# Where attention's softmax is divided by its sum: on the product with the values, or on the exponentials themselves, from the seventh pair of heads on

## The chip, the core and the metric

The kernel runs on one core of a Trainium2 chip. The engines of the core are TensorE (PE; its weight loads are listed apart as PEld), VectorE (DVE), ScalarE (ACT), GpSimd (POOL) and SyncE (SP, which here only issues DMAs). Each engine works through its own instructions in order and meets the others at semaphores. The metric is device time in microseconds (us) of one execution.

## The reference: what is computed

Inputs are q, k and v for 4 batches, 8 heads, 768 positions and 64 features. An attention that only sees keys of the same hash bucket comes first:

```python
mask = q_bucket[:, :, :, None] == k_bucket[:, :, None, :]
scores = scale * np.matmul(q, k.transpose(0, 1, 3, 2))
scores = np.where(mask, scores, -1000000000.0)
scores = scores - np.max(scores, axis=-1, keepdims=True)
attn = np.exp(scores)
attn = attn / (np.sum(attn, axis=-1, keepdims=True) + 1e-09)
return np.matmul(attn, v).astype(np.float32)
```

The heads of a batch are then joined to x, 768 by 512, and a feed-forward part follows: relu(x @ w_in), a convolution of three taps along the positions, h * sigmoid(conv), and a product with w_out.

## The kernel before

**Pairs, units, blocks.** Two heads make a pair; there are 16, four to a batch. A pair has 12 units: a unit is 128 queries of one head against all 768 keys. Four units in a row (two query tiles of both heads, 256 queries) make a block, so a pair has three.

**A unit.** On PE `products` (L250) computes the scores s into PSUM; the mask is part of that product. DVE reads s in `maximum` (L260): it clamps, copies to the SBUF tile e and takes each row's maximum; a second, tiny instruction (L262) turns the maximum into the bias st. ACT then writes exp over e in place and accumulates the row sums (`exponential`, L265). Three units later PE transposes e, 128 columns at a time, into a PSUM tile t (`transposes`, L280), and ACT copies t to SBUF as at (`to_sbuf`, L287).

**The values.** Once a block's four units are copied, PE multiplies them with v (`chunk`, L306), 12 products that the trace lists as 24 instructions. That happens in one stage of four, the one given a 7 by `AVS`.

**The division.** It stands behind the product. When a block's last sum is known, DVE adds 1e-9 and takes reciprocals of the block's four sums (`reciprocals`, L270, L271), GpSimd spreads them to a 128x256 tile rec (L274), PE turns rec with two transposes ahead of the values (`spread`, L301), and ACT copies that out of PSUM (`factors`, L311). DVE multiplies the product by it (x, L315), and GpSimd splits x into a rounded part xh (L316) and the rest xl (L317), which the feed-forward part reads.

**The order.** It is written by hand. Stage i of the main loop issues, engine by engine: s of unit i, its maximum, the transposes of unit i-3 and their copy, the exponential of unit i, then values. In this text A, B, C and D are the four stages of a block in the steady part, where D is the one that also carries the values of the block before; A is the first after them. s and t tiles share a ring of three PSUM buffers (tag S): the transposes in stage i take the buffer of s of unit i-1, so they wait for that unit's maximum; s of unit i takes that of the transposes of stage i-2, so it waits for their copy. Tiles e come from a ring of five.

**Around it.** `prepare` splits the next pair's q and k on GpSimd in the course of a pair (hi, L168; bits, L188; lo, L173, listed as R<-R,hi). In the first six pairs DVE, ACT and GpSimd also decode the weights. After pairs 6, 10, 14 and 16 the feed-forward part of one batch runs (`ffn`), with the last block's values inside it (`fill`).

## Time and profile before

| | before |
|---|---|
| median of 3 runs | 766.6 us (763.26 to 768.91) |
| the profiled execution's own time | 764.44 us |
| its span in the trace | 761.6 us |
| PE busy | 722.1 us (95%) |
| ACT busy | 511.9 us (67%) |
| DVE busy | 486.1 us (64%) |
| GpSimd busy | 294.9 us (39%) |
| granted TensorE clock, mean | 0.992 of 2.4 GHz |

The span runs from the first to the last instruction in the trace; 2.8 us of the execution's time lie around it. PE's matmuls are pipelined, and their listed durations overlap: what a matmul costs is read from one start to the next. "Idle before" in a row is the time in which the engine stood still ahead of an instruction, with what ended it behind the arrow.

### The profile page before, as it was taken

How to read it: one execution, taken by the hardware profiler on the slowest of the kernel's cores; microseconds unless marked ns; L12 is line 12 of the kernel's file. 1: busy time of each engine (PE TensorE's matmuls, PEld its weight loads, DVE VectorE, ACT ScalarE, POOL GpSimd, SP SyncE). 2: the span in 40 equal slices, each digit the busy share in tenths (PEclk: the TensorE clock that was granted, in tenths of full speed). 3: DMA queues.
4: the chain of work that ended last, by engine and by line, in shares of the span. 5: the costliest groups of instructions: out<-in, count | busy, mean ns of one | idle time of the engine just before them, and what ended most of it. 6: DMA issues, size and time to landing. Idle time of an engine off the chain costs nothing.

```text
span 761.6 us, 12950 instructions
## 1 busy us (share of the span) xinstructions
PE 722.1 (95%) x4648; PEld 595.3 (78%) x4648; DVE 486.1 (64%) x1032; ACT 511.9 (67%) x954; POOL 294.9 (39%) x325
## 2 busy tenths in 40 slices
PE   5989989888889999999999999999999999999997
PEld 3867767665679987777889988777778998778986
DVE  7789978777857555555546655555546665554663
ACT  5877768777755558777765557777775556775554
POOL 4355765566536221433424421333424421113222
PEclk8999999999999999999999999999999999999999
DMA  4666576484422111445632202256361211000011
GB/s 138 157 181 191 128 195 165 117 230 108 116 50 65 60 42 64 118 123 150 140 105 53 73 1 105 48 147 154 95 174 40 63 42 62 2 1 1 0 43 41
DMA packets 30351, 72.13 MB, mean 95 GB/s; under 512 B 5936, under 2 KB 7504, under 8 KB 30288
## 3 DMA queue, kind: packets, MB, share of 16 engines
q1 hardware_dynamic: 30000, 71.27, 34.7%
q8 instruction: 36, 0.59, 0.3%
q14 instruction: 27, 0.22, 0.1%
q10 hardware_dynamic: 288, 0.05, 0.0%
HBM read 27.40 MB, written 6.29 MB: 44 GB/s over the span
## 4 chain that ended last, share of the span: by engine, by line
PE 69%; DVE 18%; DMA 5%; ACT 3%; issue 2%; POOL 1%; SPq 1%; DVEq 0%; POOLq 0%; ACTq 0%
PE o L365 18%; PE h L335 17%; PE v L306 14%; PE t L280 10%; DVE e L260 9%; PE s L250 9%; DMA R<-in_qk 2%; ACT at L287 2%; DMA k<-R 2%; DVE x L315 1%; PE hash L183 1%; PE v L301 1%; DVE wuo L92 1%; DVE wlo L96 1%; DVE st L262 1%
## 5 line engine op out<-in xcount | busy, mean ns | idle before, releaser
L260 DVE TENSOR_SCALAR_CACHE_REDUCE e<-s 128x768 f32<-128x768 f32 x192 | 182.9, 953 | 108.2 <-PE s L250 100.4
L265 ACT ACTIVATE e<-e,st 128x768 f32<-128x768 f32 x192 | 180.8, 941 | 30.0 <-DVE st L262 22.2
L287 ACT COPY at<-t 128x768 f32<-128x768 f32 x192 | 151.8, 792 | 61.1 <-PE t L280 61.1
L280 PE MATMUL t<-ident,e 128*128 128x128 f32 x1152 | 161.5, 277 | 17.4 <-DVE e L260 15.2
L280 PEld LDWEIGHTS t<-ident,e 128*128 128x128 f32 x1152 | 133.0, 141 | 40.1 <-DVE e L260 33.5
L344 DVE SCALAR_TENSOR_TENSOR ht<-ht,cw 128x384 f32<-128x384 f32 (+1 forms) x128 | 113.9, 890 | 71.1 <-ACT ht L342 67.4
L365 PE MATMUL o<-wo,g 128*128 128x512 f32 x576 | 143.0, 394 | 1.0 <-POOL g L354 1.0
L335 PE MATMUL h<-xh,wi 128*128 128x386 f32 x512 | 142.2, 341 | 1.0 <-ACT ht L340 1.0
L306 PE MATMUL v<-at,v 128*64 128x256 f32 x1152 | 137.0, 383 | 0.0
L354 POOL TENSOR_TENSOR g<-ht,g 128x384 fp32r<-128x384 f32 x64 | 72.0, 1124 | 151.9 <-ACT g L353 120.1
L365 PEld LDWEIGHTS o<-wo,g 128*128 128x128 f32 x576 | 107.3, 188 | 21.9 <-POOL g L354 1.4
L250 PE MATMUL s<-K,Q 128*128 128x384 f32 x384 | 117.5, 387 | 3.7 <-DVE e L260 2.7
L274 POOL TENSOR_SCALAR rec<-sums 128x256 f32<-128x256 f32 x48 | 19.5, 406 | 246.7 <-ACT at L287 146.7
L306 PEld LDWEIGHTS v<-at,v 128*64 128x64 f32 x1152 | 82.0, 137 | 41.2 <-issue 7.9
L250 PE MATMUL s<-k,q 96*128 96x384 f32 x384 | 99.8, 341 | 2.3 <-DVE e L260 2.2
L335 PEld LDWEIGHTS h<-xh,wi 128*128 128x128 f32 x512 | 94.1, 188 | 5.0 <-ACT ht L340 1.5
L347 ACT ACTIVATE ht<-ht 128x384 f32<-128x384 f32 x64 | 33.6, 526 | 90.4 <-DVE ht L344 90.2
L335 PE MATMUL h<-xl,wi 128*128 128x386 f32 x256 | 86.8, 339 | 0.0
L250 PEld LDWEIGHTS s<-K,Q 128*128 128x128 f32 x384 | 58.9, 192 | 34.5 <-issue 19.0
L250 PEld LDWEIGHTS s<-k,q 96*128 96x128 f32 x384 | 71.1, 192 | 3.1 <-ACT q L230 3.1
L348 DVE TENSOR_TENSOR ht<-ht 128x384 f32<-128x384 f32 x64 | 43.4, 679 | 33.7 <-ACT ht L347 33.4
L173 POOL TENSOR_TENSOR R<-R,hi 128x768 fp32r<-128x768 f32 x30 | 58.9, 1964 | 0.7
(70 smaller groups left out, 632.9 us busy)
## 6 DMA issues: line engine op xcount, KB each, us to landing
R<-in_qk SPq DMA_DIRECT2D x15, 768.0 KB
K<-hi SPq DMA_DIRECT2D x60, 192.0 KB
v<-in_v SPq DMA_DIRECT2D x16, 384.0 KB
out<-osb SPq DMA_DIRECT2D x24, 256.0 KB
Q<-hi SPq DMA_DIRECT2D x30, 192.0 KB
q<-hi SPq DMA_DIRECT2D x30, 192.0 KB
Q<-R SPq DMA_DIRECT2D x30, 192.0 KB
k<-R SPq DMA_DIRECT2D x30, 192.0 KB
```

What stands on the lines that cost most here:

```text
L173: nc.gpsimd.tensor_tensor(lo, R, hi.bitcast(F32), ALU.subtract)
L250: nc.tensor.matmul(self.sp[:, half, :HS], A[:, h, qs], C[:, h, half * HS:(half + 1) * HS], start=(kk == 0), stop=(kk == 1))
L260: nc.vector.tensor_scalar(self.e.rearrange("p (a b) -> p a b", a=2), self.sp[:, :, :HS], MASKED, None, ALU.max, ALU.max, accum_out=self.st ...
L265: nc.scalar.activation(self.e, self.e, AF.Exp, bias=self.st[:, 1:2], scale=SCALE, accum_out=self.sums[:, self.tq, self.h:self.h + 1])
L280: nc.tensor.transpose(self.tp[:, c // 3, c % 3 * P:(c % 3 + 1) * P], self.e[:, c * P:(c + 1) * P], ident)
L287: nc.scalar.copy(pr.at[self.h][:, :, :, self.tq * P:(self.tq + 1) * P], self.tp[:, :, :3 * P].rearrange("p j (c q) -> p j c q", c=3))
L306: nc.tensor.matmul(av[h * D:(h + 1) * D, :QB], vt[:, c, h, :], ats[h][:, c // 3, c % 3, :], start=(c == 0), stop=(c == NCK - 1), tile_posi ...
L335: nc.tensor.matmul(hp[:, :HW], w, x[:, c0:c0 + HW], start=(n == 0), stop=(n == 3 * NCC - 1))
L344: nc.vector.scalar_tensor_tensor(t[:, a:z], ht[:, o + k - 1 + a:o + k - 1 + z], cw[:, f, k:k + 1], t[:, a:z], ALU.mult, ALU.add)
L348: nc.vector.tensor_tensor(t, ht[:, o:o + HS], t, ALU.mult)
L354: nc.gpsimd.tensor_tensor(g[:, 1, :], t, g[:, 0, :].bitcast(F32), ALU.subtract)
L365: nc.tensor.matmul(op, l, r, start=(f == 0 and n == 0), stop=(f == NFC - 1 and n == 2))
```

## The change

`LATE = NP + DEFER` is 6: pairs 0 to 5 are left as they were, pairs 6 to 15 (120 units, 30 blocks) are "late". In a late pair

- the row sum goes to a third column of the unit's st tile, and `total` adds 1e-9 to it on DVE, one instruction a unit, placed one stage later, between the next unit's maximum and that unit's bias;
- `normalise` takes the reciprocal of the unit's sum on DVE and multiplies e by it in place on GpSimd (128x768), also one stage later, after the next unit's exponential;
- `reciprocals` (with rec) and `spread` are gone;
- the product is copied out of PSUM by ACT as xh, rounded, and DVE subtracts it from the product to give xl; the copy of the factors, x, and GpSimd's two instructions of the split are gone.

```diff
+LATE = NP + DEFER
-        def maximum(self):
+        def maximum(self, prev):
...
+            self.sum = self.st[:, 2:3] if pr.late else pr.sums[:, self.tq, self.h:self.h + 1]
...
             nc.vector.tensor_scalar(self.e.rearrange("p (a b) -> p a b", a=2), self.sp[:, :, :HS],
                                     MASKED, None, ALU.max, ALU.max, accum_out=self.st[:, 0:1])
+            if prev and prev.pair.late:
+                prev.total()
             nc.vector.tensor_scalar(self.st[:, 1:2], self.st[:, 0:1], -SCALE, None, ALU.mult)
...
+        def total(self):
+            nc.vector.tensor_scalar(self.sum, self.sum, 1e-9, None, ALU.add)
+
+        def normalise(self):
+            nc.vector.reciprocal(self.st[:, 3:4], self.sum)
+            nc.gpsimd.tensor_scalar(self.e, self.e, self.st[:, 3:4], 0.0, ALU.mult, ALU.add)
...
+        def out_high():
+            nc.scalar.copy(xh[:, cols], av[:, :QB])
+
+        def out_low():
+            nc.vector.tensor_tensor(xl[:, cols], av[:, :QB], xh[:, cols].bitcast(F32), ALU.subtract)
...
+        if pr.late:
+            return chunks, (out_high, out_low)
...
+        prev = units[i - 1] if 1 <= i <= n else None
...
-            u.maximum()
+            u.maximum(prev)
+        elif prev and prev.pair.late:
+            prev.total()
...
-        if two and two.tq == QB // P - 1 and two.h == 1:
+        if two and not two.pair.late and two.tq == QB // P - 1 and two.h == 1:
             two.reciprocals()
...
         if u:
             u.exponential()
+        if prev and prev.pair.late:
+            prev.normalise()
```

On DVE, in stages A to C of the last block of a late pair, this stood before (a unit is named pair, tile, head: e_1_4_0 is its tile, and v_1_0 the product of the pair's first block):

```order
L260 TENSOR_SCALAR e_1_4_0_4164,st_1_4_0_4162<-s_1_4_0_4157 128x768
L262 TENSOR_SCALAR st_1_4_0_4162<-st_1_4_0_4162 128x1
L260 TENSOR_SCALAR e_1_5_0_4182,st_1_5_0_4181<-s_1_5_0_4176 128x768
L262 TENSOR_SCALAR st_1_5_0_4181<-st_1_5_0_4181 128x1
L270 TENSOR_SCALAR sums_1_2_0_4046<-sums_1_2_0_4046 128x4
L271 RECIPROCAL sums_1_2_0_4046<-sums_1_2_0_4046 128x4
L315 TENSOR_TENSOR x_1_0_4198<-v_1_0_4111,rs_1_0_4112 128x256
L260 TENSOR_SCALAR e_1_4_1_4208,st_1_4_1_4207<-s_1_4_1_4202 128x768
```

And on DVE at the same place this stands now:

```order
L266 TENSOR_SCALAR e_1_4_0_4184,st_1_4_0_4183<-s_1_4_0_4178 128x768
L277 TENSOR_SCALAR st_1_3_1_4138<-st_1_3_1_4138 128x1
L270 TENSOR_SCALAR st_1_4_0_4183<-st_1_4_0_4183 128x1
L280 RECIPROCAL st_1_3_1_4138<-st_1_3_1_4138 128x1
L266 TENSOR_SCALAR e_1_5_0_4205,st_1_5_0_4204<-s_1_5_0_4199 128x768
L277 TENSOR_SCALAR st_1_4_0_4183<-st_1_4_0_4183 128x1
L270 TENSOR_SCALAR st_1_5_0_4204<-st_1_5_0_4204 128x1
L280 RECIPROCAL st_1_4_0_4183<-st_1_4_0_4183 128x1
L339 TENSOR_TENSOR xl_1_4131<-v_1_0_4132,xh_1_4130 128x256
L266 TENSOR_SCALAR e_1_4_1_4227,st_1_4_1_4226<-s_1_4_1_4221 128x768
```

Each stage has two more small instructions of the unit before, and stage B has lost the two on the block's sums; xl stands where x stood.

On GpSimd, the same pair's first block and its turn to the second read before:

```order
L168 TENSOR_SCALAR hi_2_0_3960<-R_2_3810 128x768
L188 TENSOR_SCALAR bits_2_3971<-bits_2_3971,cst 128x384
L173 TENSOR_TENSOR R_2_3810<-R_2_3810,hi_2_0_3960 128x768
L274 TENSOR_SCALAR rec_1_1_1_4070<-sums_1_0_0_3921 128x256
L316 TENSOR_SCALAR xh_0_3767<-x_0_2_4081 128x256
L317 TENSOR_TENSOR xl_0_3768<-x_0_2_4081,xh_0_3767 128x256
L168 TENSOR_SCALAR hi_2_1_4085<-R_2_3810 128x768
```

And on GpSimd there now:

```order
L171 TENSOR_SCALAR hi_2_0_3977<-R_2_3828 128x768
L281 TENSOR_SCALAR e_1_1_0_3961<-e_1_1_0_3961,st_1_1_0_3960 128x768
L191 TENSOR_SCALAR bits_2_3988<-bits_2_3988,cst 128x384
L281 TENSOR_SCALAR e_1_0_1_3996<-e_1_0_1_3996,st_1_0_1_3995 128x768
L176 TENSOR_TENSOR R_2_3828<-R_2_3828,hi_2_0_3977 128x768
L281 TENSOR_SCALAR e_1_1_1_4027<-e_1_1_1_4027,st_1_1_1_4026 128x768
L281 TENSOR_SCALAR e_1_2_0_4066<-e_1_2_0_4066,st_1_2_0_4065 128x768
L171 TENSOR_SCALAR hi_2_1_4103<-R_2_3828 128x768
```

Three instructions a block are gone, and one on a whole e tile stands in every stage, with the split of the next pair in between as before.

On PE, in stage D of the middle block, this stood before (t is the transposed tile):

```order
L280 MATMUL t_1_4_0_4231<-ident,e_1_4_0_4164 128x128 x6
L301 MATMUL v_1_1_4220<-ident,rec_1_3_1_4187 128x128 x2
L306 MATMUL v_1_1_4220<-at_1_1_0_4129,v_1_3808 64x256
```

And now on PE:

```order
L296 MATMUL t_1_4_0_4253<-ident,e_1_4_0_4184 128x128 x6
L322 MATMUL v_1_1_4242<-at_1_1_0_4150,v_1_3826 64x256
```

The two transposes of rec are gone; nothing else moved on PE.

## Rows read from the trace of the kernel before

**Rows 1.** Busy us (count) of PE, PEld, DVE, ACT, POOL; clock; DMA; 302-385 us

```profile
302.00:385.00 83.00, 82.27 (x623) 64.97 (x622) 46.36 (x139) 62.89 (x117) 30.96 (x42) 1.00 0.53 134
```

**Rows 2.** Timeline of PE, one block: start, duration, operation

```profile
338.77 0.62 PE L250 MATMUL s<-K,Q 128*128 128x384 f32 x2
...
339.59 0.82 PE L280 MATMUL t<-ident,e 128*128 128x128 f32 x6
...
342.29 0.83 PE L280 MATMUL t<-ident,e 128*128 128x128 f32 x6
342.91 0.62 PE L250 MATMUL s<-K,Q 128*128 128x384 f32 x2
...
343.93 0.87 PE L280 MATMUL t<-ident,e 128*128 128x128 f32 x6
344.64 0.38 PE L301 MATMUL v<-ident,rec 128*128 128x128 f32 x2
344.95 2.81 PE L306 MATMUL v<-at,v 128*64 128x256 f32 x24
347.69 0.61 PE L250 MATMUL s<-K,Q 128*128 128x384 f32 x2
```

**Rows 3.** Timeline of the weight loads, same block, with idle time before

```profile
342.25 0.64 PEld L280 LDWEIGHTS t<-ident,e 128*128 128x128 f32 x6
...
343.93 0.64 PEld L280 LDWEIGHTS t<-ident,e 128*128 128x128 f32 x6 [0.36 <-DVE e L260]
```

**Rows 4.** Timeline of DVE, same block, stages A to C

```profile
339.79 0.96 DVE L260 TENSOR_SCALAR_CACHE_REDUCE e<-s 128x768 f32<-128x768 f32 x1 [3.37 <-PE s L250]
...
340.79 0.15 DVE L262 TENSOR_SCALAR st<-st 128x1 f32<-128x1 f32 x1
341.23 0.96 DVE L260 TENSOR_SCALAR_CACHE_REDUCE e<-s 128x768 f32<-128x768 f32 x1 [0.29 <-PE s L250]
...
342.30 0.16 DVE L270 TENSOR_SCALAR sums<-sums 128x4 f32<-128x4 f32 x1
342.50 0.18 DVE L271 RECIPROCAL sums<-sums 128x4 f32<-128x4 f32 x1
...
342.92 0.94 DVE L260 TENSOR_SCALAR_CACHE_REDUCE e<-s 128x768 f32<-128x768 f32 x1
```

**Rows 5.** Timeline of ACT, same block: the exponentials of units A and B

```profile
341.14 0.94 ACT L265 ACTIVATE e<-e,st 128x768 f32<-128x768 f32 x1
341.98 0.19 ACT L265 ACTIVATION_READ_ACCUMULATOR e<-e,st 128x1 f32 x1
...
342.75 0.94 ACT L265 ACTIVATE e<-e,st 128x768 f32<-128x768 f32 x1
```

**Rows 6.** Eighteen transposes in a row after the last unit, timeline of PE

```profile
684.62 2.18 PE L280 MATMUL t<-ident,e 128*128 128x128 f32 x18
686.56 0.42 PE L335 MATMUL h<-xh,wi 128*128 128x386 f32 x1
```

**Rows 7.** GpSimd's groups by line, 302 to 385 us: busy, mean ns

```profile
L173 POOL TENSOR_TENSOR R<-R,hi 128x768 fp32r<-128x768 f32 x6 | 11.0, 1837 | 0.2
...
L168 POOL TENSOR_SCALAR hi<-R 128x768 fp32r<-128x768 f32 x6 | 5.0, 832 | 0.0
...
L274 POOL TENSOR_SCALAR rec<-sums 128x256 f32<-128x256 f32 x9 | 3.6, 405 | 50.7 <-ACT at L287 45.5 <-PE t L280 5.2
...
L188 POOL TENSOR_SCALAR bits<-bits,cst 128x384 fp32r<-128x384 f32 x3 | 1.7, 583 | 0.0
```

**Rows 8.** Timeline of GpSimd: rec, behind the reciprocal of rows 4

```profile
342.86 0.40 POOL L274 TENSOR_SCALAR rec<-sums 128x256 f32<-128x256 f32 x1 [4.82 <-ACT at L287]
```

**Rows 9.** DVE's bias instruction (L262), all 192: duration ns least/median/most

```profile
L262 DVE TENSOR_SCALAR st<-st x192: 152/154/156, 11.0 to 681.9; 128x1 f32<-128x1 f32 x192
```

**Rows 10.** Timeline of DVE, second maximum after a feed-forward part

```profile
284.46 0.96 DVE L260 TENSOR_SCALAR_CACHE_REDUCE e<-s 128x768 f32<-128x768 f32 x1
```

**Rows 11.** Timeline of PE, first transposes that wait after that part

```profile
285.48 0.88 PE L280 MATMUL t<-ident,e 128*128 128x128 f32 x6
```

More of the change, by code (lines that the diff above doesn't have):

```diff
@@ L145, in __init__ @@
             self.b, self.p, self.nm = b, p, f"{b}_{p}"
+            self.late = b * NP + p >= LATE
+            self.rec = None
         def load(self):
@@ L251, in products @@
                                      start=(kk == 0), stop=(kk == 1))
-        def maximum(self):
-            self.st = ring(wp, 8, [P, 2], F32, "st", f"st{self.nm}")
-            if self.tq == 0 and self.h == 0:
-                self.pair.sums = ring(wp, 3, [P, QB // P, 2], F32, "sums", f"sums{self.nm}")
-            self.sums = self.pair.sums
+        def maximum(self, prev):
+            self.st = ring(wp, 8, [P, 4], F32, "st", f"st{self.nm}")
+            pr = self.pair
+            if self.tq == 0 and self.h == 0 and not pr.late:
+                pr.sums = ring(wp, 3, [P, QB // P, 2], F32, "sums", f"sums{self.nm}")
+            self.sums = None if pr.late else pr.sums
+            self.sum = self.st[:, 2:3] if pr.late else pr.sums[:, self.tq, self.h:self.h + 1]
             e = wp.tile([P, 776], F32, tag="e", name=f"e{self.nm}", bufs=EB)
@@ L265, in exponential @@
             nc.scalar.activation(self.e, self.e, AF.Exp, bias=self.st[:, 1:2], scale=SCALE,
-                                 accum_out=self.sums[:, self.tq, self.h:self.h + 1])
+                                 accum_out=self.sum)
+        def total(self):
[3 more added lines that the diff above has]
+            nc.gpsimd.tensor_scalar(self.e, self.e, self.st[:, 3:4], 0.0, ALU.mult, ALU.add)
         def reciprocals(self):
-            nc.vector.tensor_scalar(self.sums, self.sums, 1e-9, None, ALU.add)
-            nc.vector.reciprocal(self.sums, self.sums)
             pr = self.pair
+            sums = self.sums
+            nc.vector.tensor_scalar(sums, sums, 1e-9, None, ALU.add)
+            nc.vector.reciprocal(sums, sums)
             pr.rec = ring(wp, 1, [P, QB // P, 2, D], F32, "rec", f"rec{self.nm}")
-            nc.gpsimd.tensor_scalar(pr.rec, self.sums.unsqueeze(3).to_broadcast([P, QB // P, 2, D]), 1.0, 0.0,
+            nc.gpsimd.tensor_scalar(pr.rec, sums.unsqueeze(3).to_broadcast([P, QB // P, 2, D]), 1.0, 0.0,
                                     ALU.mult, ALU.add)
@@ L317, in out @@
             nc.gpsimd.tensor_tensor(xl[:, cols], x, xh[:, cols].bitcast(F32), ALU.subtract)
+        def out_high():
+            nc.scalar.copy(xh[:, cols], av[:, :QB])
+        def out_low():
+            nc.vector.tensor_tensor(xl[:, cols], av[:, :QB], xh[:, cols].bitcast(F32), ALU.subtract)
+        cols = slice(qb * QB, (qb + 1) * QB)
+        chunks = [lambda c=c: chunk(c) for c in range(NCK)]
+        if pr.late:
+            return chunks, (out_high, out_low)
         rs = ring(wp, 2, [P, QB], F32, "rs", f"rs{pr.nm}_{qb}")
-        cols = slice(qb * QB, (qb + 1) * QB)
-        return [spread, *(lambda c=c: chunk(c) for c in range(NCK))], (factors, out)
+        return [spread, *chunks], (factors, out)
     g2, prep = [None], [iter(())]
```

## The prediction, made before the changed kernel was run

> **What bounds the kernel now.** I read the busy time over a stretch of late pairs without a feed-forward part first. PE is busy for 82.3 of 83 us at full granted clock, ACT for 62.9, DVE for 46.4, GpSimd for 31.0 [rows 1]. So what the change does to PE's row counts, and the other engines matter where PE waits for them. Busy is not the same as issuing, though, so I read PE from start to start in one block [rows 2]. Stages A, B and C take (342.91 - 338.77) / 3 = 1.38 us each; stage D takes 4.78, to 347.69, the block 8.92. In A the transposes follow the start of s by 0.82 us, in D by 1.02: PE loses 0.20 us there, and the weight load names DVE as what it waited for [rows 3]. It is stage C's maximum, which ends at 342.92 + 0.94 = 343.86 and frees the PSUM buffer that stage D's transposes take; it began 1.69 us after stage B's, since the block's sums, reciprocals and x stand between [rows 4]. So a block is PE's work plus 0.20 us for DVE. The change touches both terms.
>
> **The change, part by part.**
>
> *Removed on PE.* Two transposes a block. Eighteen in a row take 686.56 - 684.62 = 1.94 us, 0.108 each [rows 6]; the listed 273 ns of one overlaps its neighbours. The step from the two transposes to the values is 0.31 us [rows 2], of which 2 x 0.108 = 0.216 are theirs; the other 0.09 belongs to the first value product and stays. Ten late pairs of three blocks are 30 blocks: 30 x 0.216 = 6.5 us. Nothing else runs on PE in that slot, so this is a gain unless a new wait fills it.
>
> *Added on DVE.* Two small instructions a unit: total like the addition of 1e-9 (0.16 us, next start 0.20 later because the reciprocal needs it), and a reciprocal (0.18, next start 0.09 later by the step to x) [rows 4]. Gone are the same two once a block; xl has the form of x (one PSUM, one SBUF input, 128x256), and I cost the exchange at nothing. In stage A the bias starts at 340.79. With total in front of it and the reciprocal behind, the next maximum could begin at about 340.79 + 0.07 + 0.20 + 0.10 = 341.16, and now begins at 341.23, when PE's scores are there [rows 4]: hidden, with 0.07 to spare; without that cover each of stages A and C would cost up to 0.3 us. In stage B the added pair takes the place of the removed pair, so stage C's maximum starts no later than now, and D's 0.20 us stays. Total in stage B waits for the exponential of unit A, which ends at 341.98 + 0.19 = 342.17 [rows 5]; stage B's maximum ends at 341.23 + 0.96 = 342.19 [rows 4]. They meet within 0.02 us, so I take no wait. Behind total on DVE stand the bias, for which ACT waits, and the next maximum, for which PE waits: this meeting is the one I trust least.
>
> *Added on GpSimd.* One 128x768 multiplication a unit, in place, with a factor per partition. The trace has no such row. The nearest: hi, 128x768 with constants, 832 ns; bits, the same two operations with the factor per partition, 583 ns at 384 columns; rec, with constants, 405 ns at 256 [rows 7]. From hi and rec a column costs (832 - 405) / 512 = 0.834 ns, which gives 512 ns at 384; bits takes 71 ns more. As a fixed surcharge that makes 0.90 us at 768, as a share (14%) 0.95. I take 0.93. Bounds: 0.83 (hi) below, 1.84 (the two-input subtraction R<-R,hi) above; it has one tile input like hi and bits, so it lies at the lower end. The Trainium skill speaks against putting it there: "GPSIMD Engine Reference", section 4.1, sends elementwise work on a tile to VectorE, and section 3.1 gives 1.8 cycles an element at 1.2 GHz as the best case of a GpSimd loop. By it the multiplication would be an estimated 1.15 us, and the sum would end at about 765 us instead of the number below; hi's 832 ns is already faster than that, so here the trace disagrees.
>
> *The new wait.* Transposes now wait for GpSimd. The tightest unit is D's: its total stands behind stage A's maximum, and its transposes are due in stage C. Stage A's maximum starts at 339.79, total at 340.79 (where the bias starts now), the reciprocal 0.20 to 0.27 later [rows 4], GpSimd 0.36 after the reciprocal's start (342.50 to 342.86) [rows 4, 8], so at 341.35 to 341.42; plus 0.93 that is 342.28 to 342.35, and the handover. The load of those transposes begins at 342.25 now [rows 3]. PE is 0.05 to 0.15 us late in C. But D's transposes cannot start before 343.93 anyway: lateness up to 0.20 us is swallowed by the stall already there. For unit A the same chain starts at total in stage B, 342.25, and ends at 343.75 to 343.85, against 343.93: just in time. So I cost the wait at nothing, with 0.20 us a block as its cover.
>
> *GpSimd's queue.* A block adds 4 x 0.93 and drops three instructions. A pair holds 12 x 0.93 + 2 x (1.84 + 0.83) + 0.58 = 17.1 us in about 27 [rows 7]. The split of the next pair is interleaved; its long instruction falls into stage D, where no multiplication is urgent.
>
> *After a feed-forward part* (three times before late units) no values cover the chain. The second maximum starts at 284.46; total and reciprocal of the held unit now stand in front of it, the reciprocal starting at about 284.56; plus 0.36 and 0.93 is 285.85 against transposes at 285.48 [rows 10, 11]: 0.4 us late, 3 x 0.4 = 1.2 us.
>
> *The last unit's* chain runs under the 2.74 us of values of its stage D [rows 2]; without that cover it would cost about 1.5 us, once.
>
> **Sum.** 764.4 (the profiled execution) - 6.5 + 1.2 = 759.1 us. That execution is 2.2 us under the median of 766.6, so against the median: 761.3 us, 0.7% faster.
>
> **The rivals.**
>
> *The stall goes too.* If stage C's maximum starts 0.20 us earlier, because total slips in under the maximum's last step, D loses nothing: 30 x 0.20 = 6.0 more, 755.3 us. For it: the block's two instructions on sums leave stage B. Against it: two others come in at the same place, and total cannot start before 342.17 [rows 5].
>
> *GpSimd's latency eats the gain.* The chain to stage C may be late by 0.20 (swallowed) plus 0.216 before the gain is gone. That is a multiplication of 342.25 + 0.42 - 341.38 = 1.28 us, or a shorter one with slow handovers: 764.4 + 1.2 + 2.2 = 767.8 us. For it: the form was never measured. Against it: hi and bits agree on 0.90 to 0.95 [rows 7]. The skill's 1.15 us would go most of this way.
>
> *DVE and ACT in lockstep (slower).* Total makes DVE wait for ACT's exponential, the bias behind it makes ACT wait for DVE. ACT's pace in A to C is one unit in 342.75 - 341.14 = 1.61 us [rows 5], slower than PE's 1.38; now it runs behind and catches up in D. If DVE can no longer run ahead of it, stages A to C take 1.61: 3 x 0.23 = 0.69 more, less the 0.20 and the 0.216, 0.27 a block, 8.2 in all: 764.4 + 8.2 + 1.2 + 2.2 = 776.0 us. It decides where exponentials end over 0.2 us later than stage B's maximum. Against it: A's and B's do not, and ACT enters A with its backlog done.
>
> *GpSimd as slow as with two inputs (slower).* At 1.84 us the chain to C ends 341.38 + 1.84 = 343.22, 0.97 late; less 0.42, that is 0.55 a block: 764.4 + 16.5 + 1.2 + 2.2 = 784.3 us at least. It is slower by 1% from about 1.54 us on. The same if GpSimd and DVE held each other up: DVE's bias takes 152 to 156 ns in all 192 cases, whatever GpSimd was doing [rows 9]. The Trainium skill, "SBUF — State Buffer", section "Who interferes with whom", says that a VectorE tensor_scalar in a two-port mode and a GpSimd instruction block each other for a whole instruction; by rows 9 the small ones here do not.
>
> **How the numbers follow.** Forecast 0.50 (its own range 757 to 765), stall gone too 0.14, gain eaten 0.21, lockstep 0.10, slow GpSimd 0.05. The range 754 to 770 us holds all of the first three and leaves out the last two. A measurement of this kernel tells about 1% from no change. Under 758.9 us: 0.14 and some 0.09 of the forecast, 0.23. Over 774.3: 0.12 of the last two. Between: 0.65.
>
> **What would show it.** The multiplication's duration near 0.93 us; blocks of about 8.7 us from s to s instead of 8.92; values that follow the transposes of stage D with nothing between; D's transposes still waiting for DVE, C's at most 0.15 us for GpSimd; ACT's exponentials not waiting for the bias in A to C. I am wrong if the multiplication takes over 1.2 us, if transposes wait for GpSimd in more than one stage of a block, or if DVE stands idle on ACT's exponential in stages B and C.

## The result and the profile after

| | before | after |
|---|---|---|
| median, measured together | 765.38 us (762.79 to 768.91) | 758.27 us (754.89 to 761.04) |
| ratio, 95% interval | | 0.9913 [0.9892, 0.9933] |
| the profiled execution's own time | 764.44 us | 758.92 us |
| its span | 761.6 us | 757.1 us |
| PE / DVE / GpSimd busy | 722.1 / 486.1 / 294.9 us | 717.0 / 498.0 / 358.1 us |

The kernel is 0.9% faster: inside the range, 3.0 us under the forecast median, and on the side that was forecast. The shares of the engines over late pairs, which answer to [rows 1], show where the work went: GpSimd's 31 us have become 50, PE is still busy all the time.

The windows view of after, 302 to 385 us (columns as in [rows 1]):

```profile
302.00:385.00 83.00, 83.00 (x622) 63.79 (x618) 50.80 (x194) 63.87 (x120) 50.30 (x52) 1.00 0.53 135
```

The timeline of PE in one block of after answers to [rows 2]:

```profile
339.31 0.62 PE L253 MATMUL s<-K,Q 128*128 128x384 f32 x2
...
340.13 0.82 PE L296 MATMUL t<-ident,e 128*128 128x128 f32 x6
340.70 0.59 PE L253 MATMUL s<-K,Q 128*128 128x384 f32 x2
...
341.53 0.84 PE L296 MATMUL t<-ident,e 128*128 128x128 f32 x6
342.13 0.60 PE L253 MATMUL s<-K,Q 128*128 128x384 f32 x2
...
342.93 0.82 PE L296 MATMUL t<-ident,e 128*128 128x128 f32 x6
343.50 0.59 PE L253 MATMUL s<-K,Q 128*128 128x384 f32 x2
...
344.43 0.85 PE L296 MATMUL t<-ident,e 128*128 128x128 f32 x6
345.21 2.81 PE L322 MATMUL v<-at,v 128*64 128x256 f32 x24
347.95 0.62 PE L253 MATMUL s<-K,Q 128*128 128x384 f32 x2
```

The block takes 347.95 - 339.31 = 8.64 us; it was 8.92. In stage D the values follow the transposes directly. The step from s to t there is 344.43 - 343.50 = 0.93 us, where it was 1.02 and is 0.80 to 0.83 in A to C. The step from s to t in B is 341.53 - 340.70 = 0.83; in A and C it is 0.82 and 0.80.

Such steps are the finest measure there is here, so the experiments are compared by them. The next table gives medians over the 16 ordinary blocks behind 300 us, from start to start: s to t ("s") and t to what follows it ("t") in each stage. "Spread" is the step of the two transposes, and the last row but one holds a pair's third kind of block, in which PE also computes the next pair's hash (one block in three, median of 6).

| us | before | after | e1 | e2 | e3 | e4 | e5 | e6 | e7 | e8 | e9 |
|---|---|---|---|---|---|---|---|---|---|---|---|
| A: s, t | .81 .58 | .81 .58 | .81 .58 | .81 .58 | .81 .58 | .81 .58 | .81 .58 | .81 .58 | .81 .58 | .81 .58 | .81 .58 |
| B: s, t | .790 .575 | .829 .603 | .830 .601 | .786 .575 | .830 .601 | .830 .602 | .829 .602 | .788 .575 | .829 .602 | .829 .602 | .829 .602 |
| C: s, t | .784 .602 | .787 .577 | .788 .577 | .781 .605 | 1.160 .631 | .788 .576 | .784 .576 | .786 .605 | .782 .575 | 1.669 .630 | .788 .576 |
| D: s, t | 1.033 .711 | .934 .776 | .932 .683 | 1.028 .804 | .823 .805 | .830 .776 | .939 .775 | .891 .804 | .844 .776 | 1.175 .804 | .830 .776 |
| spread | .312 | none | .312 | none | none | none | none | none | none | none | none |
| values | 2.741 | 2.741 | 2.741 | 2.741 | 2.741 | 2.741 | 2.741 | 2.741 | 2.741 | 2.741 | 2.741 |
| block | 8.927 | 8.632 | 8.851 | 8.708 | 8.981 | 8.529 | 8.634 | 8.570 | 8.535 | 9.836 | 8.531 |
| block with hash | 9.588 | 9.507 | 9.726 | 9.368 | 9.506 | 9.521 | 9.510 | 9.364 | 9.507 | 9.761 | 9.503 |
| pair | 27.44 | 26.77 | 27.42 | 26.79 | 27.47 | 26.56 | 26.77 | 26.51 | 26.58 | 29.99 | 26.55 |

The part up to the seventh pair's first maximum has the same code in before, after and the runs e1 to e9, and yet takes 201.4 to 206.8 us from one execution to another. A difference of 2 us between two runs' times therefore says little; one of 0.03 us in a block that repeats says much.

The chain that the prediction followed, on DVE (it answers to [rows 4]; the timeline of after, stages A to C of the same block):

```profile
340.42 0.96 DVE L266 TENSOR_SCALAR_CACHE_REDUCE e<-s 128x768 f32<-128x768 f32 x1 [3.07 <-PE s L253]
341.30 0.08 DVE L266 DVE_READ_ACCUMULATOR e<-s 128x1 f32 x1
341.30 0.15 DVE L277 TENSOR_SCALAR st<-st 128x1 f32<-128x1 f32 x1
341.42 0.15 DVE L270 TENSOR_SCALAR st<-st 128x1 f32<-128x1 f32 x1
341.49 0.16 DVE L280 RECIPROCAL st<-st 128x1 f32<-128x1 f32 x1
341.77 0.96 DVE L266 TENSOR_SCALAR_CACHE_REDUCE e<-s 128x768 f32<-128x768 f32 x1
...
342.74 0.15 DVE L277 TENSOR_SCALAR st<-st 128x1 f32<-128x1 f32 x1
...
343.01 0.41 DVE L339 TENSOR_TENSOR xl<-v,xh 128x256 fp32r<-128x256 f32 x1
343.33 0.95 DVE L266 TENSOR_SCALAR_CACHE_REDUCE e<-s 128x768 f32<-128x768 f32 x1
```

On GpSimd, the same block (timeline of after):

```profile
341.82 0.92 POOL L281 TENSOR_SCALAR e<-e,st 128x768 f32<-128x768 f32 x1 [1.58 <-ACT at L303]
343.29 0.91 POOL L281 TENSOR_SCALAR e<-e,st 128x768 f32<-128x768 f32 x1 [0.55 <-DVE st L280]
```

And the weight loads of the transposes in B, C and D, with the idle time ahead of them; it answers to [rows 3]:

```profile
341.50 0.64 PEld L296 LDWEIGHTS t<-ident,e 128*128 128x128 f32 x6 [0.17 <-issue]
...
342.86 0.65 PEld L296 LDWEIGHTS t<-ident,e 128*128 128x128 f32 x6
...
344.40 0.65 PEld L296 LDWEIGHTS t<-ident,e 128*128 128x128 f32 x6 [0.28 <-POOL e L281]
```

In stage A total does not wait for the end of the maximum: it starts together with the accumulator read, at 341.30, and runs beside it. The bias follows 1.00 us after the maximum's start, as it did before. In B and C that is not so: the bias comes 1.04 and 1.10 us after the maximum's start there (medians over the ordinary blocks), where it came after 1.00 and 0.99. The multiplication runs from 341.82 to 342.74, and the load that needs it starts at 342.86, with no idle time. In D the loads are put down to GpSimd, but the multiplication for them (343.29 + 0.91 = 344.20) ended together with stage C's maximum, whose accumulator read starts at 344.20: two waits that end within the same 0.1 us, and which of them counts is what the experiments had to say. In B the idle time ahead of the load has no releaser at all ("issue").

### The profile page after: what moved, and what is told of

Read it like the earlier page. It is cut to its first block, busy times and chain, and to the rows that moved or that the text cites. A ratio compares the mean times of both kernels' runs of the same rounds, so it can differ in the third digit from the quotient of the medians.

```text
span 757.1 us, 13345 instructions
## 1 busy us (share of the span) xinstructions
PE 717.0 (95%) x4588; PEld 586.6 (77%) x4588; DVE 498.0 (66%) x1212; ACT 511.9 (68%) x954; POOL 358.1 (47%) x355
## 4 chain that ended last, share of the span: by engine, by line
PE 77%; DVE 15%; ACT 2%; DMA 2%; POOL 2%; issue 1%; DVEq 0%; SPq 0%; POOLq 0%; ACTq 0%
PE o L390 18%; PE h L360 17%; PE v L322 15%; PE s L253 13%; PE t L296 13%; DVE e L266 6%; DMA R<-in_qk 2%; PE hash L186 1%; DVE wuo L93 1%; DVE wlo L97 1%; DVE wui L93 1%; DVE st L270 1%; ACT e L273 1%; DVE wli L97 1%; DVE x L331 1%
## 5 line engine op out<-in xcount | busy, mean ns | idle before, releaser
L281 POOL TENSOR_SCALAR e<-e,st 128x768 f32<-128x768 f32 x120 | 109.2, 910 | 126.1 <-ACT at L303 65.0
L296 PEld LDWEIGHTS t<-ident,e 128*128 128x128 f32 x1152 | 130.9, 142 | 43.4 <-DVE e L266 23.7
```

Of the source, the lines that this page charges most:

```text
L281: nc.gpsimd.tensor_scalar(self.e, self.e, self.st[:, 3:4], 0.0, ALU.mult, ALU.add)
L296: nc.tensor.transpose(self.tp[:, c // 3, c % 3 * P:(c % 3 + 1) * P], self.e[:, c * P:(c + 1) * P], ident)
```

## The experiments

**e1 and e2: are the two transposes the gain?** e1 puts them back into the changed kernel, with an operand that is always there; e2 takes them out of the kernel before and does nothing else.

```diff
# e1, values() of after
+        def again():
+            for t in range(QB // P):
+                nc.tensor.transpose(av[:, QB + t * P:QB + (t + 1) * P], ident, ident)
         if pr.late:
-            return chunks, (out_high, out_low)
+            return [again, *chunks], (out_high, out_low)
# e2, values() of before
-            nc.scalar.copy(rs, av[:, QB:2 * QB])
+            nc.scalar.copy(rs, av[:, :QB] if pr.late else av[:, QB:2 * QB])
...
-        return [spread, *(lambda c=c: chunk(c) for c in range(NCK))], (factors, out)
+        return chunks if pr.late else [spread, *chunks], (factors, out)
```

> The changed kernel with two transposes put back in front of the values of each late block (of the identity, into the half of the PSUM tile that nothing reads), so that PE has the work that the change took away and everything else stays changed. Theory 1 (the gain is PE's issue time of these two transposes, 0.22 to 0.24 us a block in start-to-start times): +0.24 x 30 = about +7 us on the changed kernel's 758.3, so 765 us, and a block of 8.88 us instead of 8.64. Theory 2 (the gain comes from VectorE's relief, which shortens stage D's stall, and PE has slack): 758 to 760 us, a block of at most 8.70 us.

> The kernel before with nothing changed but this: in the ten late pairs the two transposes of the factors are left out, and the copy of the factors reads the product in their place (so the late pairs' values are squared instead of divided). Theory 1: 30 x 0.22 to 0.24 = 6.5 to 7.2 us under the kernel before, about 758.5 us, and a block of about 8.69 us instead of 8.92, with stage D's stall of 0.20 us unchanged. Theory 2 (PE's time is refilled by the wait for VectorE): 763 to 766 us, the stall of D grown by what the transposes gave.

e1: 765.38 us, ratio to before 1.0005 [0.9987, 1.0024]. e2: 758.14 us, 0.9911 [0.9880, 0.9943]. Stage D of e1 in the timeline of PE:

```profile
345.83 0.71 PE L296 MATMUL t<-ident,e 128*128 128x128 f32 x5
346.37 0.38 PE L346 MATMUL v<-ident 128*128 128x128 f32 x2
346.68 2.81 PE L322 MATMUL v<-at,v 128*64 128x256 f32 x24
```

The step 346.37 to 346.68 is the 0.31 us of [rows 2] again. From after to e1 the block grows by 8.851 - 8.632 = 0.219; from before to e2 it shrinks by 8.927 - 8.708 = 0.219. In sum the change gains what PE's two transposes are worth. Everything else that it does sums to about nothing: after is where e2 is, and e1 where before is. That sum hides several terms of both signs, which the other runs take apart.

**e3 and e8: how long may the multiplication be?** A second multiplication, by 1.0, of 256 (e3) or all 768 columns (e8) follows each late one.

```diff
             nc.gpsimd.tensor_scalar(self.e, self.e, self.st[:, 3:4], 0.0, ALU.mult, ALU.add)
+            nc.gpsimd.tensor_scalar(self.e[:, :256], self.e[:, :256], 1.0, 0.0, ALU.mult, ALU.add)
```

> The changed kernel with a second GpSimd instruction behind each multiplication: the first 256 columns of the same exponentials times 1.0, which changes no value and lengthens the chain that the transposes wait for by 0.41 us plus a handover on GpSimd, to 1.35 us in all. By the recorded sum (0.20 us of cover in stage D and 0.216 of gain, break-even at 1.28 us) the block would be back near 8.95 us and the kernel near 767 us. By the trace of the changed kernel, in which stage D's transposes already start within 0.2 us of the multiplication's end: no cover is left, each block gets 0.40 to 0.45 us longer, 9.05 us, and the kernel 758.3 + 13 = 771 us. If the multiplication has cover that neither sees: 758 to 760 us.

> A second multiplication by 1.0 of all 768 columns on GpSimd follows each late unit's first, so that the unit's chain is some .91 us longer and GpSimd has 1.8 us of work for each unit in stages of about 1.4 us. This is the rival of a slow GpSimd with a known size. With 256 columns more (.3 us) the third stage's transposes came .37 us later, and the block took 8.981. If from there each further microsecond of the chain is paid once in a block: 8.98 + .6 = 9.6, and the run at 758 + 30 x .97 = 787 us. If GpSimd's work itself now sets the pace (four units of 1.82 us, 7.3 us of a block of 8.6, with the values' 2.7 us at its end in which it catches up), the chain is paid in more than one stage: 10 to 10.5, and 800 us or more. If VectorE's operands were slowed by GpSimd's longer runs, VectorE's maxima (L266) would take over 1% more than in the changed kernel.

e3: 766.66 us, 1.0020 [1.0003, 1.0036], where the recorded sum had 767 and the reading of after's trace 771. e8: 789.51 us, 1.0344 [1.0308, 1.0380]. GpSimd's groups by line in e8, 302 to 385 us (busy, mean ns of one):

```profile
L281 POOL TENSOR_SCALAR e<-e,st 128x768 f32<-128x768 f32 x33 | 30.1, 911 | 9.1 <-ACT at L304 9.1
L282 POOL TENSOR_SCALAR e<-e 128x768 f32<-128x768 f32 x33 | 27.5, 833 | 2.8
```

In e3 the additional one takes 405 ns. The timeline of PE in e8 shows where the longer chain is paid, in stage C:

```profile
347.28 0.59 PE L253 MATMUL s<-K,Q 128*128 128x384 f32 x2
...
349.54 0.87 PE L297 MATMUL t<-ident,e 128*128 128x128 f32 x6 [1.32 <-POOL e L282]
```

With 0.41 us more the chain is paid once, in C (0.787 to 1.160), and D's wait for DVE disappears behind it (0.934 to 0.823): the gain of the change is gone. With 0.83 us more C takes 1.669 and D 1.175: a block is 1.20 us longer than in after, between the 9.6 and the 10 that were expected, and lateness is paid in two stages. DVE's maximum takes a mean of 956 ns in after and in e8 alike (31 of each, 320 to 400 us), so GpSimd's longer runs do not slow this instruction of VectorE's.

**e4 and e7: what is left of the stall in D?** e4 holds xl back until stage D. e7 leaves out the 1e-9.

```diff
# e4, main loop
...
         for high, low in done:
-            low()
+            if low.__name__ == "out_low":
+                held.append((high, low))
+            else:
+                low()
+        if i % 4 == 3:
+            for high, low in held:
+                low()
+            held = []
# e7, maximum()
-            if prev and prev.pair.late:
-                prev.total()
...
```

> The changed kernel with the subtraction that gives xl on VectorE (0.41 us) moved from stage B to stage D of late blocks, where VectorE then stands idle under the values. Stage C's maximum starts 1.56 us after stage B's now; without the subtraction it could start about 1.35 after. Theory A (stage D's transposes, 0.12 us late, wait for stage C's maximum): the wait goes, a block takes about 8.54 us, the kernel 755.3 us. Theory B (they wait for GpSimd's multiplication of unit A, which ends within 0.1 us of that maximum and does not move): the block stays at 8.60 to 8.64 us and the kernel at 757 to 758.5 us.

> The addition of 1e-9 to a late unit's sum is left out (a row's sum is at least 1, where the largest element is exp(0), so in fp32 the result is the same); the reciprocal reads the sum directly. The small operation no longer stands between the maximum's result and the scaled maximum that the exponential waits for. Theory A (the stall ahead of the fourth stage's products, .934 against .81 elsewhere, is the third stage's maximum being late on VectorE, behind xl, the addition and the reciprocal): each operation taken from VectorE there counts at its length, about .06 to .10, the fourth stage's products come to .84 to .88, the block to 8.54 to 8.58 and the run to 755.5 to 757 us. Rival: the addition runs within the maximum's own end and costs nothing: .93, 8.63, 758 us.

e4: 757.12 us, 0.9899 [0.9871, 0.9927]; block 8.529. e7: 756.13 us, 0.9911 [0.9881, 0.9940]; block 8.535. Both bring D's step from s to t down to what other stages have, 0.830 and 0.844. So it was DVE's order that made D wait, and not GpSimd, as the row of the weight loads said. e4 is the cleaner of the two: its multiplication for D's transposes ends 4.88 us after the block's start, as in after, and the transposes start 0.10 us earlier all the same (medians over the ordinary blocks); e7 also lets the multiplication start earlier. e5, below, settles it from the other side. Neither time can be told from that of after.

**e5 and e6: why does stage B take 0.07 us more?** In B the transposes come 0.04 us and the next products 0.03 us later than before, in after and in e1, e3, e4, e7 and e8 alike. Is the chain through GpSimd too long there, or is it the wait as such?

```diff
# e5
-            nc.gpsimd.tensor_scalar(self.e, self.e, self.st[:, 3:4], 0.0, ALU.mult, ALU.add)
+            nc.gpsimd.tensor_scalar(self.e[:, :8], self.e[:, :8], self.st[:, 3:4], 0.0, ALU.mult, ALU.add)
# e6
-            nc.gpsimd.tensor_scalar(self.e, self.e, self.st[:, 3:4], 0.0, ALU.mult, ALU.add)
```

> GpSimd's multiplication of a late unit's exponentials covers 8 of the 768 columns, so the weights that are transposed are not normalised; everything else, and every wait, is that of the changed kernel. In the changed kernel an ordinary block takes 8.632 us of TensorE (products, then transposes, stage by stage: .808 .575, .829 .603, .787 .577, .934 .776, values 2.741); before, the second stage had .790 .575. Theory S (the .07 us lost in the second stage are the second semaphore, GpSimd's, that the transposes' weight load now has beside VectorE's): the multiplication's length is no matter, the second stage stays at .829 .603, the block at 8.63 and the run at 758 us. Theory C (the chain total, reciprocal, multiplication of .91 us ends too late for the transposes): with a multiplication of some .1 us the second stage goes back to .79 .575, the block to 8.56 and the run to 756 us (30 blocks x .07).

> GpSimd's multiplication of the late units is left out altogether (the weights that are transposed are not normalised); total and reciprocal stay on VectorE. The transposes and the maxima that reuse the buffer then wait for no GpSimd work there. Theory S (second semaphore): the second stage goes back to .79 .575 and the block from 8.632 to 8.56; run 756 us. Theory C (length of the chain): the same 8.56 here, but also with the 8 columns. If neither holds and the second stage's time comes from the order of VectorE's work (total and reciprocal between the maxima), it stays at .829 .603 in both, and the run at 758 us.

e5: 757.94 us, 0.9924 [0.9899, 0.9949]; block 8.634. e6: 753.31 us, 0.9878 [0.9840, 0.9916]; block 8.570. The multiplication of 8 columns takes 272 ns (the rows of GpSimd's spans are rough) and changes nothing: B stays at .829 .602, the blocks with the hash at 9.510. D's step stays at .939 too, though GpSimd is done there 0.88 us before the transposes start (median), so what D waits for is DVE. Without the multiplication B is back at .788 .575 and the blocks with the hash come down to 9.364. Total and reciprocal are still there in e6, so DVE's order is not what B pays for. What costs is that there is a second engine to wait for. The view of the transposes' line shows it: a row of PE's queue for weight loads counts the semaphore instructions that stand apart from the loads (duration ns least, median, most; first and last start). After:

```profile
L296 PEld LDWEIGHTS t<-ident,e x1152: 137/140/231, 15.2 to 682.1; 128*128 128x128 f32 x192
L296 PEldq EVENT_SEMAPHORE  x113: 51/51/51, 13.5 to 677.0; - x113
```

e5, with 8 columns:

```profile
L296 PEldq EVENT_SEMAPHORE  x114: 51/51/51, 13.8 to 677.8; - x114
...
  issue: 9.6, 46
```

e6, without the multiplication:

```profile
L295 PEldq EVENT_SEMAPHORE  x3: 51/51/51, 13.5 to 678.0; - x3
...
  issue: 0.4, 1
```

Before had 3 of them too. Where transposes wait for DVE (the PSUM buffer) and for GpSimd (e), one of the two waits is an instruction of its own, of 51 ns, 113 times for 120 late units, and the loads stand idle with no releaser but their own issue 46 times in e5, once in e6. DVE has such instructions as well, ahead of the maximum, which writes a tile e that GpSimd has also written: 31 of 21 ns in before, 112 in after and in e5, 7 in e6. The view of the maximum's line in after, then in e6:

```profile
L266 DVEq EVENT_SEMAPHORE  x112: 21/21/21, 29.7 to 675.9; - x112
```

```profile
L266 DVEq EVENT_SEMAPHORE  x7: 21/21/21, 30.5 to 636.8; - x7
```

Both places show in the steps (medians over the ordinary blocks). Stage A's maximum starts 1.10 us after the start of s in after and e5, 1.01 us in before and e6. In D the transposes start 0.155 us after the end of the maximum whose buffer they take, in after, e4, e5, e7 and e9, and 0.064 us after it in before and e6. B's transposes are tied to A's maximum in the same way, 0.155 us behind its end, and it takes both delays to make their step 0.83: 1.10 + 0.96 + 0.155 - 1.38, where 1.38 is the length of stage A; by the same sum one of the two alone would make it 0.74, and the 0.79 of before and e6 would stand. No run has only one of the two, so this stays worked out and not shown.

The price of the second wait is 8.634 - 8.570 = 0.064 us an ordinary block and 9.510 - 9.364 = 0.146 a block with the hash: 20 x 0.064 + 10 x 0.146 = 2.7 us of the run. That is the largest thing that the change loses. In an ordinary block B's loss vanishes in D's wait for C's maximum, which starts 4.01 us after the block's start in after and e6 alike; the price is D's 0.09 us, of which 0.03 come back in the step behind. In a block with the hash, where D does not wait for DVE's order, B and D pay some 0.07 us each. The two medians lie 4.6 us apart, but one trace of each gives 2.3 us for the part from the seventh pair's first maximum on (551.27 us in e5, 548.98 in e6).

**e9: the three edits together.** No 1e-9, xl in stage D, and, for the last unit, reciprocal and multiplication issued ahead of the subtraction xl. Only the last of them is shown here.

```diff
...
+        if not u and prev and prev.pair.late:
+            prev.normalise()
         if ending:
...
-        if prev and prev.pair.late:
+        if u and prev and prev.pair.late:
             prev.normalise()
```

> Three edits of the changed kernel together. The 1e-9 is left out (as in the run with that edit alone: block 8.535); the subtraction xl is held back until the fourth stage (alone: block 8.529); and for the last unit, which has no unit behind it, reciprocal and multiplication are issued ahead of the subtraction xl, not behind it. Theory A (one stall of .934 - .81 = .12 ahead of the fourth stage's products, which either edit takes from): the two together can only bring the fourth stage's products to .81 to .83, so the block is 8.51 to 8.53, not 8.632 - .097 - .103 = 8.43. Rival (the edits add up): 8.43. The tail: in the changed kernel TensorE stood .86 us ahead of the last unit's transposes, which waited for the chain ACT's xh, xl, total, reciprocal, multiplication; with the chain ahead of xl it should stand at most .3 us there. Time: 758 - 30 x .1 - .6 = 754.5 us against 758 of the changed kernel; with the edits adding up 752.

e9: 757.83 us, 0.9899 [0.9871, 0.9926]; its profiled execution has a span of 751.6 us. Block 8.531: e4 and e7 removed one and the same stall, and their gains do not add up. The 754.5 us that were expected are not what the median shows. The tail, in the timeline of PE:

```profile
672.12 2.81 PE L320 MATMUL v<-at,v 128*64 128x256 f32 x24
674.86 2.19 PE L294 MATMUL t<-ident,e 128*128 128x128 f32 x18
676.80 0.42 PE L358 MATMUL h<-xh,wi 128*128 128x386 f32 x1
```

Eighteen transposes stand in a row again, as in [rows 6]; in after the last six came 0.86 us late (below). The last pair, with the feed-forward part, takes 101.26 us instead of 102.68, and the same edits do as much in e11 against e10 below (101.34 instead of 102.74). Behind the seventh pair's start the trace of e9 has 549.46 us instead of 552.60; but e10 and e12, whose late pairs are those of after, have 550.59 and 549.88 there, so one trace does not show these 3.1 us. Nor can the median of 757.83 be told from after's. e9 beats before; whether its whole time beats after's stays open.

**e10 to e12: would the first six pairs gain as well?** e10 uses the new form from the first pair on. e11 does so with e9's edits. e12 is e10 with GpSimd's multiplication left out in the first six pairs.

```diff
-LATE = NP + DEFER
+LATE = 0
```

> The new form is used from the first pair on (the constant that names the first late pair is 0), so that no unit is left with the product's division. In the early part of the changed kernel (span 0 to 204) VectorE is busy 43.65 us of 50 and GpSimd 30.52, with the weights' preparation in operations of up to 2.0 us, and TensorE waits for VectorE's maxima. Theory D (there VectorE sets the pace): each early unit brings .31 us of total and reciprocal where the old form had .34 for four, some .22 more, and GpSimd's .91 stands behind preparations of 2 us: 72 units x .1 to .22 = 7 to 16 us lost, against 18 x .22 = 4 us of spread transposes saved; time 762 to 770 us. Rival (the early part is bound by TensorE or the weights' DMAs and hides VectorE's operations): gains 18 x .22 = 4 us, 754 us.

> The three edits (no 1e-9, xl in the fourth stage, the last unit's chain ahead of xl) with the new form from the first pair on. Theory D: as with all pairs and no other edit, but each early unit adds only the reciprocal's .16 us to VectorE, against .34 for four units before, about .08 more; so the early part loses 2 to 6 us less its 4 us of spread transposes, within 3 us of the kernel with the three edits alone, 753 to 758 us. Rival: 4 us faster than that kernel, 750 us.

> As with the new form from the first pair on, but in the first six pairs GpSimd's multiplication is left out (the weights of those pairs are not normalised); total and reciprocal stay there on VectorE. With the multiplication the part up to the first maximum of the seventh pair took 223.96 us, 19.4 more than in the changed kernel (204.53), and 219.35 with the 1e-9 left out. Theory G (GpSimd's queue, which is in order: a multiplication that waits for its reciprocal holds up the preparation behind it, and preparation holds up the next multiplication and PE's transposes): the early part falls back to 202 to 208 us and the run to 755 to 762 us. Theory D (VectorE's small operations in the units' chain): the early part stays at 215 or more, the run at 768 or more. If it lies between, both have a share.

e10: 776.42 us, 1.0151 [1.0123, 1.0179]. e11: 769.72 us, 1.0069 [1.0045, 1.0094]. e12: 756.43 us, 0.9897 [0.9860, 0.9934]. The part up to the seventh pair's first maximum takes 204.53 us in after, 223.96 in e10, 219.35 in e11 and 205.54 in e12. The windows view, 20 to 204 us (PE, PEld, DVE, ACT, GpSimd), of after:

```profile
20.00:204.00 184.00, 162.12 (x1157) 126.12 (x1156) 150.31 (x341) 138.22 (x252) 105.76 (x106) 0.98 0.62 164
```

of e10:

```profile
20.00:204.00 184.00, 151.79 (x1025) 115.78 (x1022) 146.43 (x405) 123.90 (x228) 134.97 (x117) 0.93 0.55 146
```

of e12:

```profile
20.00:204.00 184.00, 163.07 (x1119) 123.39 (x1118) 152.22 (x443) 136.99 (x250) 79.12 (x58) 0.95 0.62 164
```

It got slower, as expected, but by more (19.4 us in that part, where 7 to 16 less 4 were named) and not for the reason given: DVE, which was said to set the pace, is less busy in e10 than in after. In e12 DVE does all that it does in e10, and the loss is gone: Theory G. GpSimd's queue is the place. In e10 it is busy for 135 of 184 us, and it also stands still at the head of its queue, with preparation waiting behind (waits on GpSimd in e10, 60 to 200 us: total us, times, longest):

```profile
POOL e L281 <- DVE st L280: 19.8, 19, 1.9
POOL e L281 <- ACT at L303: 9.7, 6, 4.6
```

e12 takes away GpSimd's busy time, its standing still and the waits of PE and DVE for it together, so how the loss divides among them is not shown. The mean granted clock is lower in e10 as well, 0.93 against 0.98; e12 has 0.95 and does not lose. The multiplication itself is longer there than in the late pairs (GpSimd's line in e10, 20 to 200 us: duration ns least/median/most):

```profile
L281 POOL TENSOR_SCALAR e<-e,st x61: 896/907/1382, 19.2 to 196.4; 128x768 f32<-128x768 f32 x61
```

The eight longest, 1.3 us each and more than the 0.93 us of any in after, all lie beside DVE's decoding of the weights (L89, L93, L97); no run tries that by itself.

The forecast for e11, within 3 us of e9, fell with the same theory: e9's edits give back 4.6 us of the 19.4 (the expectation of e12 puts that down to the 1e-9 alone, but e11 holds xl back too). So the limit at the seventh pair is worth 12 us (e11 against e9) to 18 us (e10 against after) by the medians, and it is GpSimd's multiplication among the weights' preparation that puts it there.

## Why the prediction came out right, step by step

**Removed on PE: right.** 0.216 us a block were worked out from eighteen transposes in a row; e1 and e2 measured 0.219 each, 6.6 us over 30 blocks against 6.5.

**The exchange on DVE: costless in stage A, "D's 0.20 us stays" wrong.** Total was put 1.00 us behind the maximum's start, where the bias stood. In stage A it starts at 0.88 (341.30 - 340.42), beside the accumulator read, and delays the bias by nothing. In stage B it is not free: without it (e7) C's maximum starts 1.46 us after B's instead of 1.56 (medians). Yet the exchange is a gain, for before these were 1.69 us, and D's step fell from 1.033 to 0.934. e2 and e6 price it: neither has the two transposes or the second wait, and e6 has all else that the change does. They lie 8.708 - 8.570 = 0.138 us apart in an ordinary block, 2.8 us over 20 of them, and not at all in the blocks with the hash (9.368 and 9.364), which have no such stall. The rival "stall goes too" was thus more than half true, 0.14 of 0.20 us, for two blocks in three; the second wait then takes nearly as much back. That the rest of the stall is DVE's order as well e4, e7 and e9 show.

**The multiplication: right.** 0.91 us against 0.93 taken. The groups by line of after in the stretch of [rows 7]:

```profile
L281 POOL TENSOR_SCALAR e<-e,st 128x768 f32<-128x768 f32 x37 | 33.7, 910 | 31.2 <-ACT at L303 20.1 <-DVE st L280 9.0 <-PE hash L186 1.1
...
L171 POOL TENSOR_SCALAR hi<-R 128x768 fp32r<-128x768 f32 x6 | 5.0, 834 | 0.0
```

e8's row with a constant, 833 ns, sets the factor per partition at 78 ns for 768 columns, against 71 ns for 384 [rows 7]: a fixed surcharge, which would have given 0.90. The Trainium skill's best case for a GpSimd loop ("GPSIMD Engine Reference", section 3.1), from which 1.15 us was estimated, is too slow for this instruction; no run here explains by what.

**The new wait: the length right, the number of waits overlooked.** The chain for stage C was to end at 342.28 to 342.35 for a load at 342.25, 0.05 to 0.15 us late. In after the load starts at 342.86 with no idle time ahead of it, and C's step is .787 against .784: not late. What failed is the sentence "so I cost the wait at nothing". It looked only for the time at which the wait ends. A second engine to wait for costs something also where its data are long there, on PE's weight loads and on DVE's maximum: 2.7 us (e5, e6).

**After a feed-forward part: too dear.** 0.4 us each were named; the place was right. The weight loads of the transposes that wait there, in the timeline of after (they answer to [rows 11]):

```profile
287.66 0.64 PEld L296 LDWEIGHTS t<-ident,e 128*128 128x128 f32 x6 [0.63 <-POOL e L281]
```

PE stands 0.32 us there, and the transposes come 0.19 us later behind their s than before (1.28 us instead of 1.09), but the step behind them gives 0.17 back. The five stages from the part's end on (284.37 to 294.35 in after, 282.36 to 292.50 in before) take 9.98 us, where they took 10.14 with one spread (0.22) in them: 0.06 us net, and the same at the other two places, 0.2 us in all where 1.2 were named.

**The last unit: wrong.** Its chain was to run under the values. In after (timeline of PE, answering to [rows 6]):

```profile
676.79 2.54 PE L322 MATMUL v<-at,v 128*64 128x256 f32 x22
679.27 1.53 PE L296 MATMUL t<-ident,e 128*128 128x128 f32 x12
681.65 0.88 PE L296 MATMUL t<-ident,e 128*128 128x128 f32 x6 [0.86 <-POOL e L281]
```

and of DVE:

```profile
679.81 0.42 DVE L339 TENSOR_TENSOR xl<-v,xh 128x256 fp32r<-128x256 f32 x1 [2.18 <-ACT xh L336]
680.15 0.14 DVE L277 TENSOR_SCALAR st<-st 128x1 f32<-128x1 f32 x1
680.33 0.16 DVE L280 RECIPROCAL st<-st 128x1 f32<-128x1 f32 x1
```

Total was free to go under the values, but stands behind xl in DVE's order, and xl waits for ACT's xh and that for the values' end. It was costed by its data and not by its queue. It cost 0.86 us once, and e9's order removes it.

**The sum.** 764.4 - 6.5 + 1.2 = 759.1 us was forecast for a profiled execution; 758.92 came out. That it is so near is in part luck. By the traces the part from the seventh pair's first maximum on, the only one that the change touches, takes 552.60 us instead of 558.74: 6.1 us less, where 5.3 were forecast. The part ahead of it, with the same code, took 1.6 us more in this execution of after (204.53 against 202.90). Of the terms, 2.8 us for the exchange on DVE and 1.0 us after the feed-forward parts were better than forecast, 2.7 us of second waits and 0.9 us at the end worse. With the 6.6 of the transposes they give 6.6 + 2.8 - 2.7 - 0.2 - 0.9 = 5.6 us; the 0.5 us to the trace's 6.1 are less than that part varies (the 550 us of e10 and e12 above). In a steady pair the terms close: 3 x 0.219 + 2 x 0.138 - 2 x 0.064 - 0.146 = 0.66, against 27.44 - 26.77 = 0.67. The forecast median was 761.3, 3.0 us too high: 1.2 because it was tied to a median of before that was that much above the later one, and 1.8 because the two medians lie 7.1 us apart, where 5.3 were forecast.

**The rivals.** *Gain eaten* was to set in at 1.28 us of multiplication, with 767.8 us; e3, at 0.91 + 0.41 = 1.32 us, measured 766.66. *Slow GpSimd*: at e8's 1.74 us the recorded working gives 764.4 + 30 x (341.38 + 1.74 - 342.25 - 0.42) + 1.2 + 2.2 = 781.3 us; 789.51 came; the recorded working has the lateness paid in C alone, and D pays as well (1.175 against 0.934). *Lockstep* did not come: total in stage B stood behind the maximum without idle time (342.74). In stage C total does wait for the exponential, some 0.07 us in an ordinary block, in one of the two stages that the prediction named as a sign of being wrong; it delays D's maximum, which has the values' time to end in, and A's step stays at 0.81. In the late pairs GpSimd and DVE did not hold each other up either: DVE's maximum takes 956 ns in after and in e8 (954 before).

## What to carry to other kernels

Work on the engine that never rests is worth its issue time, start to start, even where its listed duration overlaps; price what replaces it by three things: the length of the new chain, the place of each link in its engine's order, and the number of different engines that an instruction then waits for. When a wait's releaser is in doubt because two end together, take time from each of them in turn: here the row named GpSimd, and it was VectorE (e4 and e5). An engine that is free in one part of the program can be the full one in another, so a form that pays in the late pairs may lose more in the early ones than the late ones gain.

## What the runs showed of the hardware that was not expected

- An additional engine to wait for put a semaphore instruction of 51 ns in PE's weight-load queue, 113 times for 120 units, and one of 21 ns in DVE's queue ahead of the maximum (112, where before had 31). It cost 0.064 us in an ordinary block and 0.146 us in one with the hash, the same with 0.27 and 0.91 us of work to wait for (e5 and after), and was gone without it (e6). Transposes that waited for DVE started 0.155 us after the maximum's end with it and 0.064 us without.
- A tiny DVE instruction behind the maximum (0.15 us) started with the accumulator read in stage A and moved the next one by nothing there, though 0.20 us had been allowed for it; in stage B leaving it out brought the next maximum 0.10 us forward (e7).
- GpSimd's one-input multiplication of 128x768 takes 833 ns with a constant and 911 ns with a factor per partition, and DVE's maximum beside it takes 956 ns whether GpSimd is busy for 50 us of 83 or, in e8, for 71. In e10's early pairs, beside DVE's decoding of the weights, the same multiplication took up to 1382 ns.
